# Scores of an attention kernel on all 128 rows: two matmuls a head on parts moved by DMA, in place of three on 64 rows

## The chip, the cores and the metric

The kernel runs on one core of one Trainium2 chip. The metric is device time in microseconds (us), the median of three runs. A profile of one further execution shows what each engine does: TensorE (PE, with its weight loads as PEld), VectorE (DVE), ScalarE (ACT), GpSimd (POOL), and SyncE (SP), which issues the DMAs.

## The reference

Attention over a window of 128 positions with 4 sink positions, 4 batches of 8 heads, 768 positions, head size 64, and behind it a mixture of 8 experts over the 3072 x 512 result.

```python
def _attn_ref(q, k, v, n_sink, window):
    B, H, S, D = q.shape                       # 4, 8, 768, 64
    scores = 1.0 / np.sqrt(D) * np.matmul(q, k.transpose(0, 1, 3, 2))
    pos = np.arange(S)
    is_sink = pos[None, :] < int(n_sink)       # 4
    rel = pos[:, None] - pos[None, :]
    in_window = (rel >= 0) & (rel < int(window))   # 128
    scores = np.where(is_sink | in_window, scores, -1000000000.0)
    a = np.exp(scores - np.max(scores, axis=-1, keepdims=True))
    a = a / (np.sum(a, axis=-1, keepdims=True) + 1e-09)
    return np.matmul(a, v).astype(np.float32)

def _moe_ref(x, w_gate, w1, w2):               # x: attention, (3072, 512)
    P = np.exp(x @ w_gate - (x @ w_gate).max())
    for _ in range(8):
        P /= P.sum(1, keepdims=True) + 1e-09
        P /= P.sum(0, keepdims=True) + 1e-09
        P *= N / E
    for e in range(E):                         # 8 experts, 512 -> 1024 -> 512
        out += P[:, e:e + 1] * (np.maximum(x @ w1[e], 0.0) @ w2[e])
```

## The kernel before

A float32 product is made of products of two float32r parts: the high part is the value rounded to float32r, the low part what is left. High by high, high by low and low by high are added up in PSUM; low by low is left out. `split` (L350 to L353) makes the parts: ACT copies the value to the high part, DVE subtracts that from the value for the low part.

The first of the kernel's stages is attention, with expert 0 filled in between; behind it come the other experts, which the change does not touch. The attention works in 48 units: `units` runs over 4 batches (b), 6 blocks of 128 positions (i) and 2 halves of the heads (hh, four heads each). A loop of steps n (L662 and on) drives them as a pipeline. In step n, in this order on PE: the scores of heads 0 and 1 of unit n+1 (`scores(n + 1, 0)`), the first half of the values of unit n-1, a piece of the gate, the transposes of q and k of unit n+2 (`transpose_qk`), the transposes of the probabilities of unit n, the scores of heads 2 and 3 of unit n+1, a fill from expert 0, the second half of the values of unit n-1, more transposes of unit n, and another fill. Fills begin at step 5. PE keeps the order in which the program is written; on the other engines, and on SP's queue, a scheduler sets the order.

For a unit, `transpose_qk` turns two heads at a time, so rows 0 to 63 of a transposed piece hold one head and rows 64 to 127 the next. k goes into KT, one tile for each half of the heads, which holds a batch's six blocks side by side, each with four columns for the sinks before it (`SEG` is 4 + 128); q goes into a tile Q. `scores` reads q and k of a head on its 64 rows. Its columns are two segments, the block before and the unit's own, 264 in all (`CW`). For a pair of heads there are three matmuls a head (L469), and they stand in turns, head 0 on rows 0 to 63, head 1 on rows 64 to 127; here they are called a score group, six matmuls into two PSUM tiles `ps`:

```python
        for j, (a, c) in enumerate(((0, 0), (0, 1), (1, 0))):
            for h in hs:
                r0 = (h % 2) * D
                nc.tensor.matmul(ps[h], lhsT=Q[r0:r0 + D, a, pr, :], rhs=K[r0:r0 + D, c, pr, :],
                                 start=(j == 0), stop=(j == 2))
```

DVE then adds the mask and takes the largest value (L472), ACT takes the exponential (L475), DVE the reciprocal of the sum (L476, L477), and POOL scales (L479). PE transposes the probabilities (L490, L506), ACT and DVE split them (PT, PS), and PE multiplies with v (L526). `store_x` copies the result to xr (L538) and stores it (L540). `load_block` (L413 to L419) loads q, k and v of a block, in two buffers each; its DMAs wait on SP for a buffer to come free. `load_sinks` loads the four sink rows of v in short DMAs (vs, L401). Ahead of it all DVE clears the parts of KT that lie before the first block (L386). L600 and L616 are matmuls of expert 0, L556, L567 and L576 those of the gate; L727 and on belong to the later stages.

## Time and profile before

| | |
|---|---|
| median of 3 runs | 2172.08 us (2171.21 to 2172.58) |
| profiled execution, its own time | 2171.77 us |
| its span (first to last instruction) | 2169.8 us |
| granted TensorE clock, mean | 0.999 |
| score matmuls, L469 | 576, busy 65.4 us |
| first and last start of L469 | 8.2 and 308.0 us |
| bytes moved by DMA | 453.31 MB, mean 209 GB/s |

A busy time is the time in which at least one instruction of the engine runs. On PE matmuls are pipelined: one that takes 0.28 us in the trace can be followed by the next after 0.12 us. So the cost of a matmul is read from one start to the next. In the order of time (the timeline) neighbours of one line are merged into one row, with their number behind an x.

### The profile page before, as it was taken

The page shows a single profiled execution, that of the slowest core. Times are in us where ns is not written, and L with a number is a line of the kernel's source. Part 1 is how long each engine was busy: PE and PEld are TensorE (multiplying, and loading weights), DVE is VectorE, ACT ScalarE, POOL GpSimd, SP SyncE. Part 2 cuts the span into 40 slices and gives each one's busy share as a digit, 9 for nine tenths or more (in the row PEclk, how much of TensorE's full clock was granted, in tenths as well). Part 3 has the DMA queues.
Part 4 walks back from the last instruction along what each step waited for, and adds up shares of the span by engine and source line. Part 5 has one row for each costly group of instructions (what it writes and reads, how often), then busy time and mean ns, then how long its engine had stood idle before and what let it go on. Part 6 is the DMA issues. An engine that isn't in the chain of part 4 may idle for free.

```text
span 2169.8 us, 31963 instructions
## 1 busy us (share of the span) xinstructions
PE 2138.9 (99%) x10525; PEld 1772.4 (82%) x10525; DVE 1555.7 (72%) x2888; ACT 892.3 (41%) x1914; POOL 742.5 (34%) x963
## 2 busy tenths in 40 slices
PE   7999999999999999999999999999999999999998
PEld 5888887788888888788888888888888888888886
DVE  8878768777787776776666676666756666766666
ACT  6777763544444443433223332323342233323222
POOL 6655544233233232132223233222322222332322
PEclk9999999999999999999999999999999999999999
DMA  6333324999998987776666666667866666666662
GB/s 173 84 84 88 84 65 158 312 306 301 288 327 272 323 290 247 237 275 204 197 199 207 204 194 199 204 195 244 306 202 203 208 203 193 203 204 193 203 195 83
DMA packets 395819, 453.31 MB, mean 209 GB/s; under 512 B 99648, under 2 KB 263680, under 8 KB 394752
## 3 DMA queue, kind: packets, MB, share of 16 engines
q1 hardware_dynamic: 395648, 451.20, 66.5%
q8 instruction: 86, 1.41, 0.3%
q14 instruction: 85, 0.70, 0.1%
HBM read 313.64 MB, written 137.46 MB: 208 GB/s over the span
## 4 chain that ended last, share of the span: by engine, by line
PE 92%; DVE 4%; ACT 1%; issue 1%; POOL 1%; DMA 0%; SPq 0%; DVEq 0%; POOLq 0%; ACTq 0%
PE c L727 39%; PE o L1298 20%; PE held L1298 8%; PE held L995 7%; PE o L995 7%; PE O L526 3%; PE ps L469 2%; PE g L600 2%; PE pt L490 2%; PE o L616 1%; PE pt L430 1%; DVE T L754 0%; ACT sc L475 0%; PE O L556 0%; PE o L1357 0%
## 5 line engine op out<-in xcount | busy, mean ns | idle before, releaser
L753 ACT CAST hf<-w 128x512 fp32r<-128x512 f32 x448 | 265.3, 621 | 561.8 <-POOL w L1265 298.5
L1298 PE MATMUL o<-hf,W2q 128*128 128x512 f32 x1920 | 471.9, 389 | 0.1
L1298 PEld LDWEIGHTS o<-hf,W2q 128*128 128x128 f32 x1920 | 360.2, 188 | 75.2 <-DVE acc L1309 0.6
L727 PE MATMUL c<-T,W1q 128*128 128x512 f32 x1530 | 388.7, 390 | 0.0
L754 DVE TENSOR_TENSOR hf<-w,hf 128x512 fp32r<-128x512 f32 x448 | 329.4, 763 | 74.2 <-ACT hf L753 66.6
L727 PEld LDWEIGHTS c<-T,W1q 128*128 128x128 f32 x1530 | 286.9, 188 | 60.0 <-ACT M L1242 0.4
L1309 DVE TENSOR_TENSOR acc<-o,acc 128x512 f32<-128x512 f32 x300 | 206.2, 687 | 172.3 <-PE o L1298 172.0
L727 PE MATMUL c<-B,W1q 128*128 128x512 f32 x1134 | 278.4, 390 | 0.0
L1265 POOL TENSOR_TENSOR w<-w 128x512 f32<-128x512 f32 x64 | 82.7, 1292 | 494.9 <-DVE w L1247 481.1
L727 PEld LDWEIGHTS c<-B,W1q 128*128 128x128 f32 x1134 | 212.6, 188 | 44.1
L1246 DVE TENSOR_TENSOR w<-c,M 128x512 f32<-128x512 f32 x192 | 132.3, 689 | 139.2 <-PE c L727 134.7
L1242 ACT COPY M<-c 128x512 f32<-128x512 f32 x192 | 112.7, 587 | 249.8 <-PE c L727 249.0
L1298 PE MATMUL held<-hf,W2q 128*128 128x512 f32 x768 | 194.8, 390 | 0.0
L727 PE MATMUL c<-T,W1f 128*128 128x512 f32 x672 | 171.5, 390 | 2.3 <-DVE C L966 2.0
L995 PE MATMUL held<-W2f,h 128*128 128x512 f32 x672 | 171.0, 390 | 0.5 <-DVE W2f L754 0.5
L995 PE MATMUL o<-W2f,h 128*128 128x512 f32 x672 | 170.6, 390 | 0.2 <-DVE acc L1002 0.2
L1298 PEld LDWEIGHTS held<-hf,W2q 128*128 128x128 f32 x768 | 144.0, 188 | 29.8
L1280 POOL TENSOR_TENSOR w<-w 128x512 f32<-128x512 f32 x64 | 106.2, 1660 | 177.7 <-DVE hf L754 177.7
L816 POOL TENSOR_TENSOR r<-r 128x256 f32<-128x256 f32 x28 | 20.8, 744 | 386.5 <-ACT M L958 228.9
L727 PEld LDWEIGHTS c<-T,W1f 128*128 128x128 f32 x672 | 125.7, 188 | 30.2 <-issue 2.4
L995 PEld LDWEIGHTS o<-W2f,h 128*128 128x128 f32 x672 | 125.9, 188 | 27.1 <-DVE acc L1002 1.0
L995 PEld LDWEIGHTS held<-W2f,h 128*128 128x128 f32 x672 | 125.9, 188 | 26.9 <-DVE W2f L754 0.9
(205 smaller groups left out, 3136.2 us busy)
## 6 DMA issues: line engine op xcount, KB each, us to landing
W2q<-w2s SPq DMA_DIRECT2D x448, 256.0 KB
W1q<-w1s SPq DMA_DIRECT2D x444, 256.0 KB
w1s<-W1f SPq DMA_DIRECT2D x56, 896.0 KB
w2s<-WT SPq DMA_DIRECT2D x136, 256.0 KB
r<-in_moe_w_dram SPq DMA_DIRECT2D x64, 512.0 KB
w2s<-W2f SPq DMA_DIRECT2D x56, 256.0 KB
PB<-psd SPq DMA_DIRECT2D x16, 512.0 KB
w2s<-W2f SPq DMA_DIRECT2D x56, 128.0 KB
```

What stands on the lines that cost most here:

```text
L469: nc.tensor.matmul(ps[h], lhsT=Q[r0:r0 + D, a, pr, :], rhs=K[r0:r0 + D, c, pr, :], start=(j == 0), stop=(j == 2))
L526: nc.tensor.matmul(u["O"][:, pr], lhsT=x_, rhs=y_, start=(j == 0), stop=(j == len(ops) - 1))
L727: nc.tensor.matmul(ps, lhsT=w1(a, k), rhs=x[:, b, k, :], start=(start and j == 0), stop=(stop and j == len(TERMS) - 1), skip_group_check=n ...
L753: nc.scalar.copy(dst[:, 0], src)
L754: at(1, lambda: nc.vector.tensor_sub(dst[:, 1], src, f32(dst[:, 0])))
L995: nc.tensor.matmul(o, lhsT=h[c, th][:, a, off:off + P], rhs=W2F[n][:, w, c, :], start=(begin and c == 0 and j == 0), stop=(end and c == 1 ...
L1242: nc.scalar.copy(t, T["c2"])
L1246: nc.vector.tensor_add(w, T["c1"], T[m])
L1265: nc.gpsimd.tensor_sub(S3, T["A11"], T["A21"])
L1280: at(k, lambda: nc.gpsimd.tensor_sub(T["A11"], w, T["A11"]))
L1298: nc.tensor.matmul(o, lhsT=W2Q[part, n, m][:, a, k * P:(k + 1) * P], rhs=F[part, n, H_OF[m]][:, w, :], start=(j == 0 and (begin or not hol ...
L1309: nc.vector.tensor_add(sums[m, k], o, sums[m, k])
```

## The change

q and k keep their high and low parts, but for each head they are laid out over all 128 rows. A tile QKS, one for each half of the heads, has three blocks of 260 columns: block 0 for q, block 1 for k, block 2 for the low part of q. On the 64 rows on which a head stands after the transposes ("own"), they hold the high parts of q and k and the low part of q; on the other 64 rows the high part of q again, the low part of k, and zeros. One matmul with block 0 as its weights gives high by high and high by low together, a second with block 2 gives low by high. So a head has two matmuls of 128 rows and 260 columns, and a score group four. They stand head by head.

ACT and DVE write the parts into a tile QK (one copy, one subtraction of 512 columns instead of two each of 256), and six DMAs a unit bring them from there into QKS (`lay_out_qk`). QKS holds two blocks of positions, which take turns (`turn_of`); its four sink columns are copied once a batch (`copy_sinks`). The mask has two layouts, for the two turns, which makes four masks instead of three. The transposes of q and k stand one step earlier (unit n+3 in step n), their loads two (n+4); v is loaded apart. The loads and splits of expert 0's weights are written at other places, and the gate's short tile ls takes a buffer of xr.

```diff
-    SEG = SINK + P
-    CW = 2 * SEG
-    C0 = SINK
-    C1 = SEG + SINK
+    CW = SINK + 2 * P
+    turn_of = lambda b, i: slice((b * NB + i) % 2 * P, ((b * NB + i) % 2 + 1) * P)
+    place = lambda b, i: slice(SINK + turn_of(b, i).start, SINK + turn_of(b, i).stop)
...
-    KT = []
+    QKS = []
     for hh in range(2):
-        t = att1.tile([P, 2, NP, (NB + 1) * SEG], F32R, name=f"KT{hh}")
-        for w in range(2):
+        t = att1.tile([P, 2, NP, 3 * CW], F32R, name=f"QKS{hh}")
+        for h in range(2):
             for pr in range(NP):
-                nc.vector.tensor_copy(t[:, w, pr, SINK:SEG], zero)
-        KT.append(t)
+                nc.vector.tensor_copy(t[:, h, pr, CW:CW + 2 * P].rearrange("p (a c) -> p a c", a=2), zero.unsqueeze(1).broadcast_to([P, 2, P]))
+                nc.vector.tensor_copy(t[:, h, pr, 2 * CW:2 * CW + 2 * P].rearrange("p (a c) -> p a c", a=2), zero.unsqueeze(1).broadcast_to([P, 2, P]))
+        QKS.append(t)
...
-        for j, r in enumerate((kr, qr)):
+        for j, nm in enumerate(("qr", "kr")):
             for pr in range(NP):
-                nc.tensor.transpose(pt[:, j * NP + pr, :], r[:, h0 + 2 * pr:h0 + 2 * pr + 2, :].rearrange("p h d -> p (h d)"), ident)
-
-        Q = att.tile([P, 2, NP, P], F32R, name="Q")
-        K = KT[hh]
-        c1 = (i + 1) * SEG + SINK
-        split(K[:, :, :, c1:c1 + P], pt[:, 0:NP])
-        split(Q, pt[:, NP:])
-        if i == 0:
-            kv = K.rearrange("p w a (s c) -> p (w a) s c", c=SEG)
-            nc.vector.tensor_copy(kv[:, :, :, 0:SINK], f32(kv[:, :, 1:2, SINK:2 * SINK]).broadcast_to([P, 2 * NP, NB + 1, SINK]))
-        u.update(Q=Q)
+                nc.tensor.transpose(pt[:, 2 * pr + j, :], raws[nm, b, i][:, h0 + 2 * pr:h0 + 2 * pr + 2, :].rearrange("p h d -> p (h d)"), ident)
+
+        QK = att.tile([P, 10, P], F32R, name="QK")
+        pq = pt.rearrange("p (r a) t -> p r a t", a=2)
+        hi = QK[:, 0:6].rearrange("p (r x) t -> p r x t", x=3)[:, :, 0:2]
+        nc.scalar.copy(hi, pq)
+        nc.vector.tensor_sub(QK[:, 2:10].rearrange("p (a c) t -> p c a t", c=4)[:, 0:4:3], pq, f32(hi))
+        u.update(QK=QK)
+
+    def lay_out_qk(n):
+
+        b, i, hh = units[n]
+        QK = f32(us[n]["QK"])
+        rows = (slice(0, D), slice(D, P))
+        for h in range(2):
+            own, other = rows[h], rows[1 - h]
+            at_ = lambda r: f32(QKS[hh][r, h]).rearrange("p a (x c) -> p a x c", x=3)[:, :, :, turn_of(b, i)]
+            nc.sync.dma_start(at_(own).rearrange("p a x c -> p (a x) c"), QK[own, 0:6])
+            nc.sync.dma_start(at_(other)[:, :, 1], QK[own, 6:10:3])
+            nc.sync.dma_start(at_(other)[:, :, 0], QK[own, 0:4:3])
+
+    def copy_sinks(n):
+
+        b, i, hh = units[n]
+        if i == 0:
+            c0 = CW + turn_of(b, i).start
+            nc.vector.tensor_copy(QKS[hh][:, :, :, CW - SINK:CW], f32(QKS[hh][:, :, :, c0:c0 + SINK]))
...
-        Q, K = u["Q"], KT[hh][:, :, :, i * SEG:(i + 2) * SEG]
+        t = QKS[hh]
+        K = t[:, :, :, CW - SINK:CW + 2 * P]
+        Q, Z = (t[:, :, :, x * CW:(x + 1) * CW][:, :, :, turn_of(b, i)] for x in (0, 2))
...
-        for j, (a, c) in enumerate(((0, 0), (0, 1), (1, 0))):
-            for h in hs:
-                r0 = (h % 2) * D
-                nc.tensor.matmul(ps[h], lhsT=Q[r0:r0 + D, a, pr, :], rhs=K[r0:r0 + D, c, pr, :],
-                                 start=(j == 0), stop=(j == 2))
         for h in hs:
-            nc.vector.tensor_tensor_reduce(out=sc[:, h, :], in0=ps[h], in1=masks[min(i, 2)], op0=ALU.add, op1=ALU.min,
+            for j, w in enumerate((Q, Z)):
+                nc.tensor.matmul(ps[h], lhsT=w[:, h % 2, pr, :], rhs=K[:, h % 2, pr, :], start=(j == 0), stop=(j == 1))
+        for h in hs:
+            nc.vector.tensor_tensor_reduce(out=sc[:, h, :], in0=ps[h], in1=masks[place(b, i).start, min(i, 2)], op0=ALU.add, op1=ALU.min,
...
-        ls = att1.tile([2 * E, GT], F32, name="ls")
+        ls = att.tile([P, KC, P], F32, name="xr").rearrange("p k t -> p (k t)")[0:2 * E, 0:GT]
...
-        for n in range(-2, L + 3):
+        for n in range(-4, L + 3):
             on = lambda j: 0 <= j < L
-            if on(n + 2):
+            if on(n + 4) and units[n + 4][2] == 0:
+                with (tc.high_priority() if n == -4 else nullcontext()):
+                    load_block(*units[n + 4][:2], ("kr", "qr"))
+            if on(n + 2) and units[n + 2][2] == 0:
                 b, i, hh = units[n + 2]
-                if hh == 0:
-                    with (tc.high_priority() if n == -2 else nullcontext()):
-                        load_block(b, i)
-                    if i == 0:
-                        load_sinks(b)
+                load_block(b, i, ("vr",))
+                if i == 0:
+                    load_sinks(b)
...
+            for n0, f in ((0, load_plain), (2, split_w1), (3, split_w2)):
+                if n in (n0, n0 + 1):
+                    f(n - n0)
...
-            for j in (0, 1) if n == -2 else (n + 2,) if n >= 0 else ():
-                if on(j):
-                    transpose_qk(j)
+            if on(n + 3):
+                transpose_qk(n + 3)
             if on(n):
                 transpose_p(n, 0)
                 split_v(n)
             if on(n + 1):
                 scores(n + 1, 1)
+            if on(n + 2):
+                copy_sinks(n + 2)
+            if on(n + 3):
+                lay_out_qk(n + 3)
```

Three places show how the change stands on the engines. First PE, in a step of the steady stretch, from the transposes of one unit's probabilities over a score group to the next; before the change:

```order
L490 MATMUL pt<-ident,sc 128x128 x4
L506 MATMUL pt<-ident,SS_166 80x128
L616 MATMUL o<-W2f,h_1227 128x512 x3
L469 MATMUL ps<-KT_173,Q 128x264 x6
L526 MATMUL O<-PT,V 128x256 x6
L526 MATMUL O<-PS,VS_1655 128x256
L556 MATMUL O<-wg_raw,xr 128x8
L430 MATMUL pt<-ident,kr 128x128 x2
L430 MATMUL pt<-ident,qr 128x128 x2
L490 MATMUL pt<-ident,sc 128x128 x4
L469 MATMUL ps<-KT_173,Q 128x264 x6
```

and with the change:

```order
L507 MATMUL pt<-ident,sc 128x128 x4
L523 MATMUL pt<-ident,SS_171 80x128
L638 MATMUL o<-W2f,h_1270 128x512 x3
L487 MATMUL ps<-QKS_182 128x260 x4
L543 MATMUL O<-PT,V 128x256 x6
L543 MATMUL O<-PS,VS_1694 128x256
L573 MATMUL O<-wg_raw,xr 128x8
L431 MATMUL pt<-ident,qr 128x128 x2
L431 MATMUL pt<-ident,kr 128x128 x2
L507 MATMUL pt<-ident,sc 128x128 x4
L487 MATMUL ps<-QKS_182 128x260 x4
```

The score groups shrink from six matmuls to four; all else stands in the same order, with q and k of the next unit but one replaced by those of the unit after that.

Second SP's queue, in the steady stretch, from the store of one block's xr to the next; before:

```order
L540 DMA xscr<-xr 128x4x128
L419 DMA kr<-in_k_dram 128x8x64
L419 DMA qr<-in_q_dram 128x8x64
L419 DMA vr<-in_v_dram 128x8x64
L540 DMA xscr<-xr 128x4x128
```

and with the change, where QKS_173 is the tile of the first half of the heads and QKS_182 that of the second:

```order
L557 DMA xscr<-xr 128x4x128
L448 DMA QKS_173<-QK 64x6x128
L449 DMA QKS_173<-QK 64x2x128
L450 DMA QKS_173<-QK 64x2x128
L448 DMA QKS_173<-QK 64x6x128
L449 DMA QKS_173<-QK 64x2x128
L450 DMA QKS_173<-QK 64x2x128
L421 DMA kr<-in_k_dram 128x8x64
L421 DMA qr<-in_q_dram 128x8x64
L421 DMA vr<-in_v_dram 128x8x64
L448 DMA QKS_182<-QK 64x6x128
```

Twelve DMAs of two units' layouts now stand between two stores, with the loads of the next block between the two units.

Third DVE at the start of the program, from the clearing to the first score group; before:

```order
L386 CAST KT_168<-zero 128x128 x4
L386 CAST KT_173<-zero 128x128 x4
L312 CAST wgr<-zero 128x128 x4
L315 TENSOR_TENSOR sel<-ident 16x8
L353 TENSOR_TENSOR KT_168<-pt,KT_168 128x2x128
L353 TENSOR_TENSOR KT_173<-pt,KT_173 128x2x128
L439 CAST KT_168<-KT_168 128x28x4
L353 TENSOR_TENSOR Q<-pt,Q 128x256 x2
L439 CAST KT_173<-KT_173 128x28x4
L472 ISA sc,st<-ps,mask_79 128x264
```

and with the change, from the last two of its sixteen clearing copies:

```order
L385 CAST QKS_182<-zero 128x256
L386 CAST QKS_182<-zero 128x256
L309 CAST wgr<-zero 128x128 x4
L312 TENSOR_TENSOR sel<-ident 16x8
L437 TENSOR_TENSOR QK<-pt,QK 128x2x2x128 x2
L407 TENSOR_TENSOR vm<-vs_220,bd 80x256
L410 CAST VS_335<-vm 80x256
L411 TENSOR_TENSOR VS_335<-vm,VS_335 16x256
L457 CAST QKS_173<-QKS_173 128x4x4
L489 ISA sc,st<-ps,mask_79 128x260
```

Between the split of q and k (L437) and the first group's mask (L489) now stand the layout's DMAs and the copy of the sink columns (L457), which waits for them.

More of the change, by code (lines that the diff above doesn't have):

```diff
@@ L269, in tile_sink_attention_moe @@
     attc = early.enter_context(tc.tile_pool(name="attc", bufs=1))
-    masks = []
-    for t in range(3):
-        m = attc.tile([P, CW], F32, name=f"mask{t}")
+    masks = {}
+    for b, i in sorted({(b_ * NB + i_) % 2 * NB + min(i_, 2): (b_, i_) for b_ in range(B) for i_ in range(NB)}.values()):
+        m = masks[place(b, i).start, min(i, 2)] = attc.tile([P, CW], F32, name=f"mask{len(masks)}")
         nc.gpsimd.memset(m, 0.0)
-        nc.gpsimd.memset(m[:, SEG:C1], NEG)
-        cur, prev = m[:, C1:CW], m[:, C0:SEG]
+        cur, prev = m[:, place(b, i)], m[:, place(b, i + 1)]
         nc.gpsimd.affine_select(out=cur, in_=cur, pattern=[[-1, P]], compare_op=ALU.is_ge, fill=NEG,
                                 base=0, channel_multiplier=1)
-        if t == 0:
+        if i == 0:
             nc.gpsimd.memset(prev, NEG)
-            nc.gpsimd.memset(m[:, C1:C1 + SINK], NEG)
+            nc.gpsimd.memset(cur[:, 0:SINK], NEG)
         else:
@@ L607, in plain_g1, with plain_g2 @@
         yield
-    def plain_g2(W, hs, us_, g, th):
+    def plain_g2(hs, us_, g, th):
         for t in range(GH // P):
@@ L631, in plain @@
         for us_ in ((0, 1), (2, 3)):
-            W = {u: load_plain(0, u) for u in us_}
             for g in range(NG):
@@ L644, in plain @@
                         hs.append(h)
+                        if us_[0] == 0 and (g, th) == (NG - 1, 1):
+                            split_w1(u + 2)
                     for _ in second:
                         yield
-                    second = plain_g2(W, hs, us_, g, th)
+                    if us_[0] == 2 and (g, th) == (0, 0):
+                        split_w2(2)
+                        split_w2(3)
+                    second = plain_g2(hs, us_, g, th)
+                    if us_[0] == 0 and (g, th) == (0, 0):
+                        load_plain(2)
+                        load_plain(3)
         for _ in second:
```

44 lines of the change are left out of this document (23 added, 21 removed).

## The prediction

> **What bounds the kernel now.** I read the page's busy times first, then a table by stretch of the part that the change touches, then its waits, and last the order of time on TensorE. A "unit" below is one block of 128 rows for four heads; there are 48, and each has two score groups (one for each pair of heads).
>
> ```profile
> span 2169.8 us, 31963 instructions
> PE 2138.9 (99%) x10525; PEld 1772.4 (82%) x10525; DVE 1555.7 (72%) x2888; ACT 892.3 (41%) x1914; POOL 742.5 (34%) x963
> ```
>
> TensorE is busy nearly always, but matmuls overlap in this count, so the stretches have to be looked at. In the next view each row is a stretch: its length, busy time of PE, weight loads, DVE, ACT and POOL with instruction counts, clock, DMA share, GB/s.
>
> ```profile
> core 0: us, PE busy (x) PEld busy (x) DVE busy (x) ACT busy (x) POOL busy (x), PEclk, DMA share, GB/s
> 0.00:8.00 8.00, 2.68 (x8) 1.16 (x8) 4.40 (x23) 2.67 (x5) 6.29 (x33) 1.00 0.73 165
> 8.00:20.00 12.00, 8.97 (x43) 6.62 (x43) 9.86 (x42) 5.98 (x22) 8.26 (x20) 1.00 0.66 157
> 20.00:56.00 36.00, 31.55 (x234) 25.56 (x233) 33.28 (x113) 30.46 (x95) 24.92 (x57) 1.00 0.63 178
> 60.00:300.00 240.00, 237.54 (x1900) 203.15 (x1899) 190.85 (x704) 176.55 (x567) 144.66 (x348) 1.00 0.33 81
> ```
>
> From 20 to 56 us VectorE sets the pace (33.28 of 36.00 us, 92%), and PE idles 4.45 us. From 60 to 300 us PE sets it: it idles 2.46 us of 240, with DVE at 80% and ACT at 74%. The waits of 60 to 320 us agree. These are two of the longer ones that PE and its weight loads have for another engine (us in all, times, longest):
>
> ```profile
> PEld ps L469 <- ACT PT L352: 5.1, 14, 0.4
> PE pt L490 <- POOL sc L479: 1.0, 2, 0.6
> ```
>
> Some 5 us in 260 is little. So in the steady stretch a microsecond taken from PE's own work should be a microsecond of time, until DVE's share nears that of the early stretch.
>
> **Score groups on PE.** Rows of the order of time: start, length, line, tiles, count.
>
> ```profile
> 206.91 0.60 PE L490 MATMUL pt<-ident,sc 128*128 128x128 f32 x4
> 207.44 0.63 PE L469 MATMUL ps<-KT,Q 64*128 64x264 f32 x6
> 208.00 0.98 PE L600 MATMUL g<-B,W 128*128 128x256 f32 x6
> 208.81 0.87 PE L526 MATMUL O<-PT,V 128*128 128x256 f32 x6
> 209.52 0.28 PE L526 MATMUL O<-PS,VS 80*128 80x256 f32 x1
> 209.64 0.60 PE L490 MATMUL pt<-ident,sc 128*128 128x128 f32 x4
> 210.08 0.27 PE L506 MATMUL pt<-ident,SS 128*80 128x128 f32 x1
> ```
>
> What counts is start to next start. The six 64-row matmuls of a group take 208.00 - 207.44 = 0.56 us, 0.093 each. Six 128-row matmuls of 256 columns take 209.52 - 208.81 = 0.71 us, 0.118 each; a 64-row one is shorter though it streams 264 columns, so the two heads of a pair do overlap. But the group also makes its neighbours longer. Four transposes take 0.44 us ahead of L506 (209.64 to 210.08) and 0.53 ahead of L469 (206.91 to 207.44): 0.09 at the entry. Six matmuls of L600 behind L469 take 0.81 (208.00 to 208.81) against the 0.71 of L526 behind L600: 0.10 at the exit. A group costs 0.09 + 0.56 + 0.10 = 0.75 us.
>
> After: four 128-row matmuls of 260 columns. Estimate 0.118 x 260/256 = 0.120 each, 0.48 together; no 64-row matmul stands beside others any more, so I take no entry and no exit cost. Saved: 0.27 us a group. Bounds: if both gaps stay, 0.67 and 0.08 saved; if the new matmuls ran at the 0.093 of the old, 0.38 saved. I take 0.27, whose rows are the nearest in shape.
>
> ```profile
> L469 PE MATMUL ps<-KT,Q x576: 274/283/587, 8.2 to 308.0; 64*128 64x264 f32 x192
> 56.00:320.00 264.00, 51.42 (x480) 34.16 (x480) 1.00 0.31 76
> ```
>
> The first row is line L469 as a whole, from its first to its last start; the second is the stretch table for this line alone. 480 of its 576 matmuls, 80 groups in 40 units, lie behind 56 us, where PE is the bound; a unit takes (308 - 56)/40 = 6.3 us. 80 x 0.27 = **-21.6 us**. The 16 earlier groups lie where DVE is the bound, and I count nothing for them.
>
> The Trainium skill has a rule that speaks against this change: TensorE: Matmul & The Clock Gate, section "Part 3: Packing small matmuls", says that matmuls on different row groups run at the same time, starting some 4 ns apart. TensorEngine Tiling (Array Packing), section "Key Properties", has the other half, that a change of tiling mode drains TensorE. By the first alone a pair costs one stream and the change loses; the trace shows both, and the measured 0.75 us holds them together.
>
> **DVE and ACT.** Rows of the groups: line, shape, count, busy us, mean ns.
>
> ```profile
> L353 DVE TENSOR_TENSOR PT<-pt,PT 128x512 fp32r<-128x512 f32 x80 | 55.0, 687 | 8.1 <-ACT PT L352 6.2
> L353 DVE TENSOR_TENSOR KT<-pt,KT 128x256 fp32r<-128x256 f32 x48 | 19.8, 413 | 4.1 <-ACT KT L352 4.1
> L353 DVE TENSOR_TENSOR Q<-pt,Q 128x256 fp32r<-128x256 f32 x48 | 19.8, 415 | 0.1
> L352 ACT CAST PT<-pt 128x512 fp32r<-128x512 f32 x80 | 46.5, 581 | 6.5 <-PE pt L490 4.9
> L352 ACT CAST Q<-pt 128x256 fp32r<-128x256 f32 x48 | 17.8, 372 | 2.4 <-DVE KT L353 2.1
> L352 ACT CAST KT<-pt 128x256 fp32r<-128x256 f32 x48 | 17.3, 360 | 9.3 <-PE pt L430 9.3
> L386 DVE CAST KT<-zero 128x128 fp32r<-128x128 f32 x8 | 1.5, 326 | 0.0
> ```
>
> Two splits of 256 columns become one of 512: on DVE 413 + 415 - 687 = 141 ns a unit less, on ACT 372 + 360 - 581 = 151 ns less. In the steady stretch this lies under PE. It matters as cover: 240 us hold 38 units, so DVE's 190.85 falls by 5.4 to 185.4, while the stretch should shrink by 76 x 0.27 = 20.5 to 219.5. DVE goes from 80% to 84%, between 80% (PE idle 1%) and the early 92% (PE idle 12%). Some new waits will come: at least 0, at most the straight line between those two points, (12 - 1) x 4/12 = 3.7% or 8 us. I take **+3**, nearer the steady row.
>
> **The added transfers.** Six DMAs a unit on SP's queue, 1280 pieces of 512 B. Rows: an xscr store alone in a window (512 such pieces), and SP's order of time.
>
> ```profile
> 120.20:122.40 2.20, 2.20 (x20) 2.20 (x19) 1.39 (x5) 2.02 (x7) 1.90 (x6) 1.00 0.37 119
> 107.56 0.37 SPq L540 DMA_DIRECT2D xscr<-xr  x1
> 109.50 0.37 SPq L419 DMA_DIRECT2D kr<-in_k_dram  x1
> 109.96 0.53 SPq L419 DMA_DIRECT2D qr<-in_q_dram  x1
> 113.30 0.37 SPq L419 DMA_DIRECT2D vr<-in_v_dram  x1
> 0.81 0.46 SPq L419 DMA_DIRECT2D kr<-in_k_dram  x1
> 3.26 0.66 PE L430 MATMUL pt<-ident,kr 128*128 128x128 f32 x2 [3.26 <-DMA kr<-in_k_dram]
> ```
>
> The store takes 0.37 x 2.2 = 0.81 us of the 16 DMA engines; 1280 pieces, 2.5 times as many, take 2.0. A unit lasts 6.3 us now, about 5.8 after, and the DMA share is 0.33, so there is room. Issue: 0.37 to 0.53 us each, six in about 2.8. From issue to use the first load takes 3.26 - 0.81 = 2.45 us. A layout is issued once the second score group of the unit two before is done, since it overwrites columns which that group reads. That is about 3 us into a step of the loop; the scores that need it stand at the start of the step after the next, 8.6 us later. 2.8 + 2.45 = 5.3, so 3.3 us are left: **0** in the steady stretch. Behind a waiting layout on SP stand the loads of q and k, with a step in hand, and the store of xr, for which nothing waits soon. The deeper pipeline (q and k split one step earlier) uses this time.
>
> **The start** has no such cover. Rows: the first score groups of units 0, 1 and 2, SP's short loads, and the last of DVE's clearing.
>
> ```profile
> 8.19 1.02 PE L469 MATMUL ps<-KT,Q 64*128 64x264 f32 x6 [1.49 <-DVE KT L439]
> 12.14 1.53 PE L469 MATMUL ps<-KT,Q 64*128 64x264 f32 x6 [0.92 <-DVE st L472]
> 18.19 1.03 PE L469 MATMUL ps<-KT,Q 64*128 64x264 f32 x6
> 6.70 4.47 SPq L401 DMA_DIRECT2D vs<-in_v_dram  x6
> 3.04 0.92 DVE L312 CAST wgr<-zero 128x128 fp32r<-128x128 f32 x4
> ```
>
> DVE now clears 8 pieces of 128 columns in 1.5 us; the change clears 16 of 256 ahead of the first split, 3 us (width free) to 6.6 (at 0.41 each, as the 256-wide splits); I take 5.3. From about 1.6 us that is 6.9, another 0.9 for wgr, 0.7 for the split: 8.5. Then five issues of 0.5 and 2.45 to land: 13.5 instead of 8.19, +5.3. Unit 1 follows behind three vs loads (2.2) and six issues (3): about 18.7 instead of 12.14. Unit 2 lands at about 21.7, instead of 18.19: +3.5. Then DVE, with 141 ns a unit less and its weight splits put into the gaps, works part of it off. I carry **+4** into the steady stretch; 1 to 6.6 are the ends. The rest of the edits I cost at 0: expert 0's weight loads are written at other places, but DVE's splits of them stand behind the same units as before (3 to 5 and 30 to 42); the fourth mask is made on POOL, which is done with its masks long before the first group; ls shares a buffer with xr twice in the program.
>
> **Sum.** -21.6 + 3 + 0 + 4 = -14.6. The profiled run took 2171.8 us (span 2169.8), 0.3 under the median shown, so the forecast is 2171.8 - 14.6 = **2157 us**. Nothing behind the attention changes but its start, and PE stays full there.
>
> **Rivals.** *DVE becomes the bound*: new waits at their 8 us or more and a start of 5 to 6: -21.6 + 8 + 6 = -7.6, about 2164, up to 2168. For it, DVE's 92% early; against it, 141 ns less a unit. *Overlap is all that counts* (the packing rule): six matmuls as three streams of 0.12, against four: 96 x 0.12 = +11.5, with the start 2187, slower. Against it: the group takes 0.56, not 0.36, by the rows above. *The layout lands late*: one chain on SP, from a group's end through six issues to landing. It has 8.6 us; each microsecond beyond costs 40 steady units or more a microsecond, so the gain is eaten at 14.6/40 = 0.4 over, at a chain of 9.0. With issues of 0.75 (as vs) and a landing of 5 it is 9.5: +36 - 14.6, about 2193. Against it: issues of 0.37 to 0.53. *The gaps stay* (they belong to the change between transposes and other matmuls): 80 x 0.08 = 6.4 less 4: 2169. Against it: 209.52 to 209.64 and 210.08 show no gap at such a change.
>
> **Chances.** Forecast (2150 to 2163) 0.60, DVE as bound 0.18, a free start and under 2150 0.05, gaps stay 0.05, layout late 0.09, overlap alone 0.03. A measurement here tells 0.2% from no change, 4.3 us. Faster: 0.60 + 0.18 + 0.05 + a part of the gaps case = 0.85; same 0.04; slower 0.11. The range takes in the forecast, the DVE case and the near side of the gaps case: 2149 to 2169.
>
> **What would show it.** Right: score groups of four at 0.48 us with 0.44 in front of and 0.71 behind them; the first group near 13.5 us; the last group some 14 us earlier than 308; no wait of PE for a QKS transfer behind 30 us. Wrong: PE waiting for QKS in every unit, groups near 0.56 or longer, DVE over 90% in 60 to 300 us, or a first group behind 18 us.

## The result, and the profile after

The changed kernel takes **2204.64 us** (median of 4 runs, 2203.23 to 2205.38) beside 2172.33 for the kernel before: ratio 1.0148, interval 1.013 to 1.0165. It is 32 us slower; the prediction was 2157, with a range of 2149 to 2169. The profiled run's span is 2201.4 us.

All of the loss lies in the attention. In the changed kernel TensorE's last unit starts at 337.94 us:

```profile
337.94 0.64 PE L487 MATMUL ps<-QKS 128*128 128x260 f32 x4
```

and in the kernel before at 305.49:

```profile
305.49 0.63 PE L469 MATMUL ps<-KT,Q 64*128 64x264 f32 x6
```

32.4 us apart, as the totals are. The starts of the units (first matmul of a unit's first score group, from the order of time) tell where. New batches begin at units 12, 24 and 36, and their disturbance lasts about three units:

| stretch | before, us | after, us | difference |
|---|---|---|---|
| start, to unit 12 | 83.2 | 95.8 | +12.6 |
| batch starts: units 12 to 14, 24 to 27, 36 to 39 | 49.2 | 68.7 | +19.5 |
| steady: units 14 to 24, 27 to 36, 39 to 47 | 173.0 | 173.4 | +0.4 |

The cost of the score groups on TensorE came out as predicted. The order of time of the changed kernel, TensorE (start, length, line, tiles, count):

```profile
154.94 0.64 PE L487 MATMUL ps<-QKS 128*128 128x260 f32 x4
155.41 0.88 PE L543 MATMUL O<-PT,V 128*128 128x256 f32 x6
...
156.39 0.41 PE L431 MATMUL pt<-ident,qr 128*128 128x128 f32 x2
156.64 0.38 PE L431 MATMUL pt<-ident,kr 128*128 128x128 f32 x2
157.06 0.63 PE L507 MATMUL pt<-ident,sc 128*128 128x128 f32 x4
157.44 0.72 PE L487 MATMUL ps<-QKS 128*128 128x260 f32 x4
158.00 0.87 PE L622 MATMUL g<-B,W 128*128 128x256 f32 x6
158.71 0.28 PE L573 MATMUL O<-wg_raw,xr 128*128 128x8 f32 x2
```

The first group of four takes 155.41 - 154.94 = 0.47 us. The second, behind the transposes of the probabilities, takes 158.00 - 157.44 = 0.56, but the four transposes ahead of it take 0.38 where they had taken 0.53, and the six matmuls of L622 behind it 0.71 instead of 0.81. From the start of these transposes to the end of L622 that is 158.71 - 157.06 = 1.65 us, against 208.81 - 206.91 = 1.90 in the prediction's rows. So most of the 0.27 us is there for this kind of group too (0.25 in this pair of rows), though in the neighbours and not in the group itself. The sign "groups near 0.56 or longer" would have misled here. But TensorE doesn't get to use it. The stretch table, six steady units (41 to 47) of the changed kernel; columns: length, then busy time of PE, PEld, DVE, ACT, POOL, granted clock, DMA share, GB/s:

```profile
298.30:337.90 39.60, 36.22 (x285) 34.03 (x284) 30.64 (x106) 27.37 (x84) 20.96 (x55) 1.00 0.79 167
```

and the same units of the kernel before:

```profile
267.10:305.50 38.40, 38.40 (x315) 33.18 (x314) 30.76 (x110) 28.01 (x89) 22.80 (x55) 1.00 0.19 49
```

TensorE has 2.2 us less to do and is idle for 3.4. What VectorE waits for in the same stretch, by the view of waits (sum, times, longest), in the changed kernel:

```profile
DVE st L493 <- ACT sc L492: 6.8, 11, 0.8
DVE W2f L350 <- ACT W2f L349: 0.7, 1, 0.7
DVE QK L437 <- DMA QKS<-QK: 0.3, 1, 0.3
```

(3.8 us, six times, for st in the kernel before). VectorE's 30.64 us of work and some 8 of waits fill 39 of the 39.6 us: VectorE sets the pace, not by its work but by waiting in line. No transfer is in that list but for 0.3 us. TensorE's matmuls in turn wait for VectorE alone, most of all for the copy of xr (all their waits here are 3.3 us):

```profile
PE O L543 <- DVE xr L555: 1.9, 2, 1.2
PE ps L487 <- DVE xr L555: 0.6, 1, 0.6
```

A batch start, SP's issues in order of time:

```profile
176.69 0.67 SPq L421 DMA_DIRECT2D qr<-in_q_dram  x1
177.45 0.67 SPq L421 DMA_DIRECT2D vr<-in_v_dram  x1
178.17 4.30 SPq L401 DMA_DIRECT2D vs<-in_v_dram  x6
182.59 0.66 SPq L448 DMA_DIRECT2D QKS<-QK  x1
...
185.98 0.60 SPq L450 DMA_DIRECT2D QKS<-QK  x1
```

and TensorE, whose previous work was issued at 186.16:

```profile
191.12 1.23 PE L487 MATMUL ps<-QKS 128*128 128x260 f32 x4 [4.03 <-DVE QKS L457]
```

TensorE stands for 4 us until VectorE's copy of the sink columns (L457). Two things stand ahead of that copy. Six loads of sink rows hold SP for 4.3 us ahead of the layout that the copy needs. And on VectorE the splits of these sink rows (vm, VS) stand ahead of it:

```profile
186.04 0.59 DVE L407 TENSOR_TENSOR vm<-vs,bd 80x256 f32<-80x256 f32 x1
...
190.38 0.42 DVE L411 TENSOR_TENSOR VS<-vm,VS 16x256 fp32r<-16x256 f32 x1
190.83 0.24 DVE L457 CAST QKS<-QKS 128x16 fp32r<-128x16 f32 x1
```

The row of the copy shows no wait for a transfer, and VectorE works for 4.5 of the 4.8 us from 186.04 on. It is the same at units 13 and 37 (copies at 110.36 and 273.00). By the semaphore updates that the trace holds, the transfers that the copy needs had landed 1.2, 2.9 and 1.8 us before it ran, at units 13, 25 and 37. So in this kernel it is VectorE's line that ends last. (The profile puts TensorE's wait at unit 37 down to a transfer, but that unit's layout had landed by 271.43.) At unit 13 there are four 512 KB loads of expert 0's weights as well, issued at 90.14 to 91.89, just ahead of the loads of k, q and v:

```profile
92.95 2.21 SPq L421 DMA_DIRECT2D qr<-in_q_dram  x1
95.26 4.24 SPq L421 DMA_DIRECT2D vr<-in_v_dram  x1
99.54 4.15 SPq L401 DMA_DIRECT2D vs<-in_v_dram  x6
```

```profile
102.00 0.69 PE L431 MATMUL pt<-ident,qr 128*128 128x128 f32 x2 [4.74 <-DMA qr<-in_q_dram]
...
103.62 1.22 PE L487 MATMUL ps<-QKS 128*128 128x260 f32 x4
104.64 1.00 PE L622 MATMUL g<-B,W 128*128 128x256 f32 x6
```

The score group behind this stop takes 104.64 - 103.62 = 1.02 us instead of 0.47 to 0.56: TensorE's granted clock is 0.50 there. Behind the stop at unit 25, too, the stretch table has 6 us at half the clock:

```profile
191.10:197.10 6.00, 5.98 (x28) 5.98 (x29) 2.47 (x11) 2.56 (x8) 0.94 (x2) 0.50 0.90 183
197.10:203.10 6.00, 6.00 (x51) 5.87 (x50) 4.36 (x19) 4.69 (x16) 2.50 (x8) 1.00 0.57 137
```

This gives an account of the batch starts, in part an estimate. TensorE stands for 4.74 and 3.27 us at unit 13 and 4.03 and 4.01 at units 25 and 37, 16.0 in all. From the clock's rows behind these four stops it loses another 9 or so (about 18 us of work at half the clock). The score groups of eight units save 4.3. Together +21, beside the +19.5 measured. In the kernel before no stretch of these has a stop over 1.2 us or a clock below 1.00.

### The profile page after: what moved, and what is told of

It reads as the page before. It is cut to its first block, busy times and chain, and to the rows that moved or that the text cites. A ratio compares the mean times of both kernels' runs of the same rounds, so it can differ in the third digit from the quotient of the medians.

```text
span 2201.4 us, 32335 instructions
## 1 busy us (share of the span) xinstructions
PE 2131.8 (97%) x10333; PEld 1791.1 (81%) x10333; DVE 1559.8 (71%) x2848; ACT 887.2 (40%) x1866; POOL 739.9 (34%) x963
## 4 chain that ended last, share of the span: by engine, by line
PE 87%; DVE 4%; DMA 4%; SPq 1%; ACT 1%; issue 1%; POOL 1%; DVEq 0%; POOLq 0%
PE c L764 39%; PE o L1335 19%; PE held L1335 8%; PE o L1032 6%; PE held L1032 6%; DMA QKS<-QK 2%; PE O L543 2%; PE ps L487 1%; PE pt L507 1%; PE g L622 1%; PE o L638 1%; DMA qr<-in_q_dram 1%; PE pt L431 1%; DVE QK L437 0%; ACT sc L492 0%
```

## The experiments

The first theories were S (SP's queue of issues), D (the 16 DMA engines) and E (another engine); later ones are told in the expectations, of which O, the order on the engines, matters most. Times are medians where there is an interval, else one run; the kernel before took 2172.4 to 2173.6 beside them.

**Half the bytes**: from unit 4 on a layout moves 32 of its 64 rows; scores there read rows that were not laid out.

```
+            if n >= 4:
+                own, other = slice(own.start, own.start + 32), slice(other.start, other.start + 32)
```

> From unit 4 on each of the six layout DMAs moves 32 of its 64 rows (the other rows of QKS keep old data): as many issues on SP, half the packets. Theory S (SP's queue is the limit: sixteen issues of about 0.65 us in a block of two units, plus six short loads at each new batch): time stays at 2204 within 5 us, the stalls of about 4 us at the batch boundaries stay. Theory D (the 16 DMA engines are the limit, share 0.88 in 60 to 100 us): the share falls under 0.65, a unit goes from 6.3 to about 5.9 us, time 2185 or less.

2203.87: nothing gained, with the DMA share from 60 to 300 us down from 0.83 to 0.60. The DMA engines are not the limit, and an issue still takes 0.59 us with half the packets.

**No layouts** from unit 4 on (the scores read old data), and **eight issues** a unit instead of six, same bytes.

```
-            if on(n + 3):
+            if on(n + 3) and n + 3 < 4:
                 lay_out_qk(n + 3)
```

> Layout DMAs only for the first two blocks (units 0 to 3); later units use what then stands in QKS. All else is issued as before. Both theories S and D: the lag of about 12 us at unit 7 stays in part, the batch stalls go, and PE's saving of 0.27 us a group shows: 2155 to 2170. Theory E (another engine, DVE at 75 to 78 percent, stops PE whatever the transfers do): units stay at 6.2 us or more, 2178 or more.

```
-            nc.sync.dma_start(at_(own).rearrange("p a x c -> p (a x) c"), QK[own, 0:6])
+            for r in range(2):
+                nc.sync.dma_start(at_(own)[:, r], QK[own, 3 * r:3 * r + 3])
```

> The own-rows DMA is cut in two: eight issues a unit in place of six, the same packets. Theory S: each block of two units gets four more issues of 0.65 us, about 1.3 us a unit where the queue is full: 2204 plus 30 to 55 us. Theory D: the same bytes and packets, 2204 within 6 us.

2163.62 and 2250.9. Without layouts the steady stretches take 158.5 us instead of 173.4 and the batch starts 46.9 instead of 68.7, while unit 12 still begins 8.6 us later than before. It looked like SP's number of issues.

**Loads on ScalarE's queue**: q, k and v from the third block on, and the later sink rows.

```
-                nc.sync.dma_start(raws[nm, b, i][:, h0:h1, :], src[...])
+                (nc.sync if b == 0 and i < 2 else nc.scalar).dma_start(raws[nm, b, i][:, h0:h1, :], src[...])
```

> The loads of q, k and v (from the third block on) and of the sink rows (from the second batch on) are issued from ACT's queue: SP has 13 issues in a block in place of 16 and none of the six short loads at a batch boundary. Theory S: the boundary stalls at units 13, 25 and 37 (9, 4 and 4 us) mostly go and a unit comes nearer to 6.0: 2204 minus 15 to 30. Theory D: the same packets, 2204 within 6 us, unless ACT is held up by waiting loads, which would show as idle ACT ahead of a DMA.

2212.97: a miss. The loads now stand behind ScalarE's own waits (GpSimd's split of v waits 22.7 us for vr, nine times, from 60 to 300 us).

**Four layouts a unit** with the same bytes: blocks arranged so that the own rows are one transfer, and k's low and q's high parts another, for which GpSimd copies q's high parts once more. Then the sink loads on ScalarE's queue, then two pairs of weight loads issued at units 6 and 7; last, these two moves alone with six layouts.

```
-            nc.sync.dma_start(at_(other)[:, :, 1], QK[own, 6:10:3])
-            nc.sync.dma_start(at_(other)[:, :, 0], QK[own, 0:4:3])
+            nc.sync.dma_start(at_(other)[:, 0:4], QK[own, 6:10])
```

> Four layout transfers a unit instead of six, with the same bytes, the same 512 B packets and the same rows of the scores; one more GpSimd instruction a unit (the second copy of q's high parts, 256 elements a row). Theory S (SP's issues are the limit: 12 layouts of about 0.65 us and the loads of a block of two units): 12 of them fall to 8, so a steady pair of units needs some 8 us of SP's 12.4, the pair falls to 11.7 to 12.0, and the whole gives 2204 - 16 to - 28 = 2176 to 2188; the stops where a new batch begins stay at about 4 us each, since the six loads of the sink rows of v still stand ahead of the layouts on SP. Theory D (the DMA engines' packets): unchanged, 2200 to 2207. Theory E (an engine, GpSimd or DVE): the same or slower, 2204 to 2212.

> The kernel of e6_four with the loads of the sink rows of v (six at each batch) issued on ScalarE's queue. Theory S: the stops at units 25 and 37 (units of 10.4 us instead of about 6.2) go, 2 x 4 us, and part of the stop at unit 13; 6 to 12 us less than e6_four. Theory D: no difference, within 3 us.

```
-                nc.sync.dma_start(vs[r0:r0 + HH * SINK, :], ...)
+                nc.scalar.dma_start(vs[r0:r0 + HH * SINK, :], ...)
...
+            for n0, f in (..., (6, lambda u: load_plain(u + 2))):
```

> The kernel of e7_four_vs with expert 0's last two pairs of weight loads (four transfers of 512 KB) issued at the steps of units 6 and 7 again, as in the kernel before, instead of among the loads of units 11 to 13. Theory S: the rest of the stop at unit 13 (a unit of 15.2 us) goes, 4 to 8 us less than e7_four_vs; with all three edits 2160 to 2175. What is left over the kernel before is the start, about 11 us late, and what is won is 0.27 us for each score group, about 40 pairs. Theory D: above 2190.

> The changed kernel with its six layouts a unit, and only the sink rows' loads on ScalarE's queue and the two pairs of weight loads at units 6 and 7. Theory S: the stops of units 13, 25 and 37 (together about 17 us) shrink by 8 to 17 us, to 2187 to 2196, while the pairs of units between them stay at 12.4 us. Theory D: nothing, 2201 to 2207, since the same bytes go through the same 16 engines.

2199.18, 2191.99, 2190.96 (ratio 1.0082, 1.0065 to 1.0099) and 2208.2. The time up to the start of unit 13 (from that of unit 12) fell from 15.7 to 12.4 and 8.9 us, up to unit 25 from 10.8 to 9.2, up to unit 37 from 10.8 to 8.2: the loads do make part of the stops. But four issues brought 5 us, not 16 to 28. The last kernel, with six layouts, won 10.8 us at the batch starts (57.9 instead of 68.7) and lost 12.1 ahead of unit 12 (107.9 instead of 95.8). S was at best a part.

**Half the bytes with four issues**, then **the own rows alone** with two issues (no transfer to the other head's rows from unit 4 on), then these cut in two: four issues again.

```
+            if n >= 4:
+                own, other = slice(own.start, own.start + 32), slice(other.start, other.start + 32)
```

> The kernel of e8_raw (2191, DMA share about 0.9 in the attention), its layouts from unit 4 on moving 32 of the 64 rows: the same four issues a unit, half the packets; the scores of those units read rows that were not laid out. Theory D2 (with SP relieved, the 16 DMA engines have become the limit): the share falls to about 0.65 and the attention's later stretch gains what still lies between e8_raw and e3_none there (22 us over units 8 to 47): 2170 to 2182. Theory L (what is left is the chain of waits of each layout: DVE's split, four issues, landing, the copy of the sink columns): less than 4 us, 2187 to 2192.

```
-            nc.sync.dma_start(at_(other)[:, 0:4], QK[own, 6:10])
+            if n < 4:
+                nc.sync.dma_start(at_(other)[:, 0:4], QK[own, 6:10])
```

> The kernel of e8_raw with only the transfers to a head's own rows from unit 4 on: two issues a unit and 60% of the packets; the other rows of the scores are not laid out there. Theory S (SP's issues still cost): 8 to 15 us less than e8_raw, 2176 to 2183, against a smaller gain in e10_half4. Theory D2: as e10_half4, within 3 us. Theory L: two issues of 0.65 us less in the chain, so 1.3 us at each of the 24 boundaries and stops that remain at most: 3 to 8 us.

```
+                nc.sync.dma_start(at_(own)[:, 0:3], QK[own, 0:3])
+                nc.sync.dma_start(at_(own)[:, 3:6], QK[own, 3:6])
```

> The kernel of e13_two (from unit 4 on only the transfers to a head's own rows; two issues a unit, 2172), with each of these transfers cut in two: four issues a unit and the bytes of e13_two, and no transfer that waits for GpSimd's second copy of q's high parts. Theory S (the number of issues on SP's queue, 0.6 us each, sets it): back to e8_raw, 2185 to 2192. Theory G (in e8_raw it was the transfers that wait for GpSimd's copy): stays at 2170 to 2175.

2187.13, 2171.78 and 2170.69. The third is the turn: as many issues as the kernel with 2190.96, and 20 us less. Neither the number of issues nor the bytes divide fast from slow here.

**The start on GpSimd's queue**, and the same with the copy of the sink columns written at the end of its step, on the kernel with 2190.96.

```
-                nc.sync.dma_start(vs[r0:r0 + HH * SINK, :], ...)
+                (nc.gpsimd if b == 0 else nc.sync).dma_start(vs[r0:r0 + HH * SINK, :], ...)
```

> The changed kernel with the first block's load of v and the first batch's six sink loads issued on GpSimd's queue, so that SP issues unit 0's layouts after the six loads of q and k alone. If SP's queue sets the start: first score group at 13 to 13.5 us (14.9 in the changed kernel), unit 2 at 22 to 24 (26.4), and 2 to 4 us less in all, 2200 to 2203. If the splits and the landing set it: nothing at unit 2, 2204 to 2206.

> The kernel of e8_raw with the start of e11_start, the second copy of q's high parts by ScalarE in the first four units, and the copy of the sink columns queued on VectorE at the end of its step, behind the second transposes of the probabilities, instead of in its middle. Theory S and L: first group at 14 to 15 us (18.9 in e8_raw), the stops of units 13, 25 and 37 (8.9, 9.2 and 8.2 us) down by 1 to 2 us each; 2179 to 2187, still slower than the kernel before. If the copy's place doesn't matter, only the start: 2186 to 2188.

2208.0 and 2190.33 (1.0073 to 1.0106). A miss: in both the scheduler put two weight loads ahead of the layouts, and the first group came at 22.6 and 22.7 us; in the second the stops stayed.

**The other transfers moved off SP**, or their extra wait: q's second copy by ScalarE; their issues on GpSimd's queue; on ScalarE's.

```
-        nc.gpsimd.tensor_scalar(QK[:, 6:8], f32(QK[:, 0:2]), 1.0, 1.0, op0=ALU.mult, op1=ALU.mult)
+        nc.scalar.copy(QK[:, 6:8], pt[:, 0:2])
```

> The kernel of e8_raw with the second copy of q's high parts made by ScalarE out of PSUM instead of by GpSimd out of SBUF; everything else the same, nothing left out. Theory G: the layouts start earlier and the stops at units 25 and 37 go; 2172 to 2182. Theory S: 2187 to 2192, 0.4 us less wait at a layout and no more.

```
-            nc.sync.dma_start(at_(other)[:, 0:4], QK[own, 6:10])
+            (nc.scalar if n < 4 else nc.gpsimd).dma_start(at_(other)[:, 0:4], QK[own, 6:10])
```

> The kernel of e8_raw with the transfers to the other head's rows issued on GpSimd's queue (in the first four units on ScalarE's): two layout issues a unit are left on SP. Nothing is left out. Theory S: the steady units as in e13_two (a pair 11.7 us) if GpSimd, busy 62% in this stretch, bears 1.2 us a unit more: 2168 to 2178. If GpSimd's issues hold up its scaling of the probabilities: 2185 to 2200. Theory G: 2187 to 2192.

> The kernel of e8_raw with the transfers to the other head's rows issued on ScalarE's queue throughout. Theory S: if ScalarE, busy 70%, bears 1.2 us a unit more, 2168 to 2178; if its softmax instructions wait behind a transfer that waits for the scores two units before, as the loads in e4_actq did, 2195 or more. Theory G: 2187 to 2192.

2195.5, 2191.06 (1.0069 to 1.0105) and 2226.51. G falls with the first. The second is no faster in all, yet its steady units from 31 to 35 take 24.0 us instead of 25.5.

**The order.** VectorE, ScalarE and GpSimd issue in the order that the program's scheduler gives them. Their traces stand in the same order, instruction for instruction, with whole and with half bytes. They stand in another one in the kernel without layouts than in the changed kernel, and in another one with 2170.69 than with 2190.96. A steady unit on VectorE, from the changed kernel (-) to the one without layouts (+); h is the expert's activation, st the two small softmax steps that follow ScalarE's exponential, xr the attention's output:

```
 SCALAR_TENSOR_TENSOR h<-g,h 128x256
-TENSOR_SCALAR st<-st 128x2
-RECIPROCAL st<-st 128x2
 COPY xr<-O 64x256
+TENSOR_SCALAR st<-st 128x2
 ISA sc,st<-ps,mask 128x260
 ISA st 128x1
+RECIPROCAL st<-st 128x2
 TENSOR_TENSOR PT<-pt,PT 128x512
```

The copy of xr had stood behind st and now stands ahead of it. So all six layouts were kept, and the three engines held to the order of the kernel without layouts by edges that order issues and wait for nothing:

```
+    for eng, order in ((EngineType.DVE, ORDER_DVE), (EngineType.Activation, ORDER_Activation), (EngineType.Pool, ORDER_Pool)):
+        mine = [i for i in traced if i.engine == eng ...]
+        for a, c in zip(order, order[1:]):
+            tc.add_manual_dep(mine[c], mine[a].name, DependencyInfo(DependencyClass.NoSync, ...))
```

> The changed kernel with all of its six layouts a unit and nothing left out, but with the instructions of VectorE, ScalarE and GpSimd in the attention kept in the order in which they stand in e3_none; TensorE's order is the program's in both, SP's is the scheduler's. The scheduler had put 384 of VectorE's rows, 134 of ScalarE's and 144 of GpSimd's elsewhere in the changed kernel than in e3_none, and e14_cut, which is fast with four issues a unit, stands in another order than e8_raw, which is slow with four. Theory O (the order that the scheduler gives VectorE when it reckons with the added transfers: the two small softmax steps right behind ScalarE's exponential, 37 us of waits in the 240 us from 60 on against 18 to 22 in the fast ones, and the copy of the sink columns): most of the 41 us between the changed kernel and e3_none comes back, 2168 to 2182, although SP issues 16 transfers a block as before. Theory S (SP's queue after all): 2198 to 2206, or more, since VectorE then waits in an order that doesn't suit late layouts. Between them, 2182 to 2198: both.

2243.79 (ratio 1.0337, 1.0318 to 1.0355): as a whole far slower, with stops of TensorE of up to 17.3 us, while GpSimd waits for vr (30.8 us, five times, from 60 to 300 us) and VectorE for sink rows (17.9). But its units 41 to 47, by the stretch table:

```profile
338.10:373.10 35.00, 35.00 (x285) 33.71 (x284) 29.30 (x105) 27.10 (x85) 20.48 (x54) 1.00 0.77 170
```

With every transfer in place TensorE is never idle, and six units take 35.0 us instead of 39.6, as without layouts (34.7). VectorE in order of time there, and in the changed kernel:

```profile
354.55 0.42 DVE L631 SCALAR_TENSOR_TENSOR h<-g,h 128x256 fp32r<-128x256 f32 x1
355.00 0.43 DVE L558 COPY xr<-O 64x256 f32<-64x256 f32 x1
355.46 0.17 DVE L496 TENSOR_SCALAR st<-st 128x2 f32<-128x2 f32 x1
```

```profile
317.74 0.42 DVE L628 SCALAR_TENSOR_TENSOR h<-g,h 128x256 fp32r<-128x256 f32 x1
318.64 0.17 DVE L493 TENSOR_SCALAR st<-st 128x2 f32<-128x2 f32 x1 [0.48 <-ACT sc L492]
318.84 0.17 DVE L494 RECIPROCAL st<-st 128x2 f32<-128x2 f32 x1
319.04 0.43 DVE L555 COPY xr<-O 64x256 f32<-64x256 f32 x1
...
321.56 0.17 DVE L493 TENSOR_SCALAR st<-st 128x2 f32<-128x2 f32 x1 [0.67 <-ACT sc L492]
```

With xr first, ScalarE has finished its exponential by the time st comes up; with st first, VectorE stands for 0.5 us and copies xr late, and TensorE waits for the place in O that xr frees. Two such waits a unit became one (6.8 us to 2.9 in six units). One thing more differs: SP's order was left to the scheduler, and it moved as well (kr's load now stands ahead of both layouts of a block, and no longer between them). So this run alone doesn't part SP's order from that of the three engines; the table below does, in part.

**Order and loads together**: four layouts a unit, nothing left out, all four engines held to the order of the fast kernel with own rows cut in two, with the start and the sink rows put where they are needed, and the small work of `attention_span` held back until SP's last transfer of the attention.

```
+    for eng, order in (..., (EngineType.SP, ORDER_SP)):
...
+            with tc.issue_after(TAIL[0]):
                 span, flag = attention_span(nc, pool, n_sink, window)
```

> Every transfer of e8_raw (four layouts a unit, both the own and the other head's rows, nothing left out), with VectorE's, ScalarE's, GpSimd's and SP's instructions of the attention kept in the order in which they stand in e14_cut, which left the other head's rows out. Changed in that order: SP issues the layouts of units 0 to 2 right behind the first block's loads of q, k and v, and the sink rows of the first batch, block two's q and k and the first weights behind them; GpSimd's copies for units 0 and 1 come ahead of its splits of v; the sink rows of the later batches are loaded and split at the units that are about to use them. Theory O with S (the scheduler's order costs the steady units about 0.5 us each, SP's queue makes the stops): a steady pair of units takes 11.7 us as in e14_cut instead of 12.4 as in e8_raw, no stop at units 25 and 37, the first group at 13 to 15 us instead of 18.9; 2163 to 2175 in all. Theory T (the other head's transfers themselves cost the 20 us between e8_raw and e14_cut): steady pairs stay at 12.3 to 12.5, 2182 to 2190 by the better start alone.

2193.14 (1.0073 to 1.0101). The steady part came as theory O had it: units 41 to 47 in 34.7 us, so T falls. The rest didn't. Unit 12 begins at 106.8 us, against 83.2 in the kernel before and 95.8 in the changed one: more than the whole loss of some 20 us arises ahead of it. TensorE's granted clock is 0.86 up to there (0.98 in the changed kernel up to its unit 12); what set off the waits ahead of it is not shown. At unit 25 VectorE's copy stood in line too early, in order of time:

```profile
185.09 0.08 DVE L492 DVE_READ_ACCUMULATOR2_ANT st<- 128x1 f32 x1
188.23 0.17 DVE L459 CAST QKS<-QKS 128x16 fp32r<-128x16 f32 x1 [3.06 <-DMA QKS<-QK]
```

The last issue of the layout that it waits for, on SP:

```profile
183.97 0.83 SPq L452 DMA_DIRECT2D QKS<-QK  x1
```

188.2 - 184.0 = 4.3 us from issue to use. The order was taken from a kernel in which that transfer didn't exist. None of these kernels is faster than the kernel before with its whole work done.

Units 41 to 47 of all these kernels, from the start of the first to that of the last: length, idle time of TensorE in it, and what stands on VectorE right behind the expert's activation h in its first steady units:

| kernel | issues a unit on SP | us | idle | behind h |
|---|---|---|---|---|
| before | | 38.3 | 0 | xr |
| changed; half the bytes | 6 | 39.7; 39.6 | 3.4; 3.2 | st |
| six, sink and weight loads moved (2208.2); start on GpSimd's queue (2208.0) | 6 | 40.1; 40.1 | 3.2; 3.4 | st |
| eight issues | 8 | 43.4 | 5.3 | st |
| four issues; sink loads moved; weight loads too (2190.96); half the bytes | 4 | 38.6; 38.8; 38.8; 38.9 | 1.8; 2.2; 2.2; 2.2 | st |
| four, start and copy moved (2190.33); q's second copy by ScalarE | 4 | 38.8; 39.6 | 2.2; 3.3 | st |
| loads on ScalarE's queue | 6 | 37.4 | 1.4 | xr |
| other rows on GpSimd's queue; on ScalarE's | 2 | 35.5; 45.8 | 0.5; 7.1 | xr |
| no layouts; own rows, whole and cut | 0; 2; 4 | 34.8; 34.9; 34.7 | 0 | xr |
| six in the order of no layouts | 6 | 35.1 | 0 | xr |
| four in the order of own rows cut | 4 | 34.7 | 0 | xr |

All kernels with the change and with st first take 38.6 us or more. Those with xr first take 37.4 or less, with one exception: with transfers on ScalarE's queue VectorE waits 7.1 us for ScalarE's exponential. In the kernel with the other rows on GpSimd's queue all transfers are made, and the scheduler put xr first by itself. With eight issues TensorE waits for transfers as well (3.3 us for qr and 1.2 for QKS in this stretch), so there SP's queue does count.

## Why the prediction was wrong

**Score groups on TensorE, 0.27 us each: right.** Where nothing else holds TensorE, six units fall from 38.3 us to 35.1 or 34.7, 0.55 to 0.6 a unit, for two groups of 0.27. In the 27 steady units that makes some 14.6 us; the kernel without layouts gained 14.5 there (173.0 to 158.5). This speaks for the prediction's reading of the rule that the Trainium skill gives in TensorE: Matmul & The Clock Gate, section "Part 3: Packing small matmuls" (row groups overlap): taken alone it would have made this part a loss, and it was a gain.

**DVE's new waits, +3 (0 to 8): the step that failed in the steady units.** It was a straight line through VectorE's busy shares, on the ground that VectorE has less to do. It has (141 ns a unit less), but what counts for an engine that issues in order is what stands next to what. The scheduler's new order put st right behind ScalarE's exponential twice a unit, and VectorE's waits ate the whole 14.5 us. This is the rival "DVE becomes the bound", with a price of 15 us in place of 8 and another mechanism; its sign, VectorE over 90% busy from 60 to 300 us, never came (177.60 of 240 us, 74%). That it was the order on the engines, and neither the bytes nor six issues a unit, is shown. VectorE's order alone was not tried, and why the scheduler chose it is not shown, only that it changes with the transfers.

**Added transfers, 0 in the steady stretch: right for the steady units; the batch starts, +19.5, were left out.** In the right order six layouts a unit cost the steady units next to nothing (35.1 us against 34.8 without any, for six units). The step looked at one layout's chain alone, with 3.3 us to spare, and its terms were each too small: an issue takes 0.59 to 0.66 us, six about 3.9 instead of 2.8, and the landing 2.9 us in the median instead of 2.45 (2.2 to 6.1 from 60 to 300 us, by the semaphore updates), 4.3 from issue to use in the row of the last run. By the same sum that is 6.8 to 8.2 of the 8.6 us, so the rival "the layout lands late" was not far off. (The Trainium skill, SBUF — State Buffer, section "The DMA setup-cost knee", gives every transfer a fixed cost of some 2 us, whatever its size. The first load of the kernel before, 2.45 us, agrees with it; the 2.9 us here and the 4.3 of the last run, with the DMA engines 0.83 and 0.90 busy from 60 to 300 us, are longer.)

For the batch starts the sum had no term at all: neither the six sink loads on SP (4.3 us ahead of the layout), nor the place of the copy of the sink columns on VectorE, nor the half clock behind a stop. In the changed kernel the copy came late in VectorE's line and not for want of the layout. Where the order had it earlier, it waited for the layout: 3.06 us in the row above, and 4.1 to 5.5 at the first copy of each new batch in the kernel with six layouts in the order of no layouts. So the two limits lie close together, and taking away one alone couldn't remove the stops. Of the 11.3 us of TensorE's stops at the copy in the changed kernel some 5.8 lie behind the landing (1.2, 2.9 and 1.8 us, an estimate from the semaphore updates) and are VectorE's; the rest lies ahead of it and is SP's and the transfers'. "Behind a waiting layout on SP stand the loads of q and k, with a step in hand" was the wrong way round: layouts stood behind loads.

**The rest of the edits at 0: wrong.** Expert 0's later weight loads, written at another place, went among the loads of units 11 to 13, where SP and the DMA engines were full; issued at units 6 and 7 again they took 3.5 us off the time up to unit 13 in the kernel with four layouts, though the whole gained only 1 us.

**The start, +4: mis-sized, +12.6 by unit 12.** First group at 14.88 instead of 13.5, unit 2 at 26.4 instead of 21.7. The lag behind the kernel before is 6.7 us at unit 0, 8.2 at unit 2, 11.6 at unit 4 and 12.6 at unit 12: VectorE did not work it off, it grew. For the first group the rows show which terms were too small, on SP:

```profile
6.81 2.24 SPq L401 DMA_DIRECT2D vs<-in_v_dram  x3
9.16 0.70 SPq L450 DMA_DIRECT2D QKS<-QK  x1
...
12.64 0.63 SPq L450 DMA_DIRECT2D QKS<-QK  x1
```

SP is busy with loads up to 9.05, and the six issues end at 13.27: 4.1 us, where five issues of 0.5 were expected. TensorE's waits up to 50 us in the changed kernel, 7.9 us of them ahead of the first group:

```profile
PE ps L487 <- DMA QKS<-QK: 11.8, 4, 7.9
PE pt L431 <- DMA qr<-in_q_dram: 5.4, 3, 4.1
PE ps L487 <- DVE QKS L457: 3.4, 1, 3.4
```

The kernel that lays out the first four units alone still has 8.6 of the 12.6 us, so most of it arises there. What in it costs how much stays open: three kernels with other first issues on SP moved the first group (to 22.6, 22.7 and 13.9 us), and none had unit 4 earlier than the changed kernel (43.0, 43.3 and 44.6, beside 41.6).

## What to carry over

A change that moves work onto transfers changes the schedule of every engine whose order is decided by a scheduler. Before pricing the work, compare the order on the engine that runs fullest, and look for short instructions that now stand right behind what they wait for. Count a queue in issues per period, with the bursts (a new batch, weight loads) and not the mean, and look at the clock behind each stop. Test a suspected order by holding the engines to the other one, SP's queue with them, all else left alone.

## What the runs showed of the hardware

The issue of a layout between two places in SBUF held SP for 0.59 us in the median whether it moved 64 or 32 rows (own rows, changed kernel and half the bytes), against 0.37 us for a load or store in the kernel before (the prediction's rows at 107.56 and 109.50). Behind four loads of 512 KB the issue of a 256 KB load took 4.24 us (the row at 95.26 above). The granted clock of TensorE, 1.00 from 60 to 300 us in the kernel before, was 0.91 in each of the three stretches of 40 us that have a stop of 4 us in the changed kernel, and 1.00 in those between; two neighbouring rows of the stretch table:

```profile
140.00:180.00 40.00, 38.48 (x306) 36.42 (x306) 29.93 (x106) 27.88 (x85) 22.00 (x55) 1.00 0.88 189
180.00:220.00 40.00, 34.63 (x253) 32.66 (x252) 28.95 (x104) 24.56 (x81) 20.90 (x52) 0.91 0.74 161
```

Finer rows (those at 191.10 and 197.10 above) show where this comes from: behind the stop the clock is 0.50 for some 6 us and then 1.00 again. TensorE works all through these 6 us, so they cost it about 3 us more (an estimate from the clock), beside the 4 of the stop. The waits of 1.2 us in the steady units, three in the changed kernel, have no such stretch behind them.
